# Six wide block products and one narrow one in the second MLP product, and the denominator's 1e-6 put into z

## The chip, the cores and the metric

The kernel runs on one core of a Trainium2 chip. The metric is the device time of one execution in microseconds; the time before is the median of three executions.

## The reference, cut to what matters

One transformer-like block, in float32, on 2048 tokens of 512 channels: a linear attention with 32 heads of 16 channels, and then a token-mixing MLP (2048 tokens to 1792 hidden rows and back), each behind a layer norm and with a residual.

```python
phi_q = concat([softmax(pq), softmax(-pq)])      # 32 features for each token and head
phi_k = concat([softmax(pk), softmax(-pk)])
kv  = einsum("bhsf,bhsd->bhfd", phi_k, v)
z   = einsum("bhsf->bhf", phi_k)
num = einsum("bhqf,bhfd->bhqd", phi_q, kv)
den = einsum("bhqf,bhf->bhq", phi_q, z)[..., None] + 1e-6
h   = x + merge_heads(num / den) @ wo
u   = gelu(einsum("bsd,sf->bdf", layernorm(layernorm(h)), w1) + b1)
out = h + transpose(einsum("bdf,fs->bds", u, w2) + b2)
```

The two softmaxes of a query sum to 1 each, so its 32 features sum to 2: a constant c added to each element of z adds 2c to the denominator.

## The kernel before, in words

Every matmul has float32 precision from two parts of its operands: ScalarE (ACT) rounds a tile to its high part (`hi`), VectorE (DVE) or GpSimd (POOL) subtracts to get the low part (`lo`), and the product is hi·hi + hi·lo + lo·hi, accumulated in PSUM. PSUM has eight banks of 128x512 floats.

**The attention.** Sixteen token tiles of 128 tokens go through it one after another. For each, POOL multiplies the query features by z (tile `zB`, spread over the partitions by a matmul with ones; line 503 copies it out of PSUM, line 456 multiplies), DVE reduces that per head and makes the weights `w` that normalize the features (`s_den`, lines 465 to 471: reduce, an operation that adds 1e-6 times a feature sum, multiply, reduce, reciprocal, multiply), and POOL applies them (line 474). TensorE (PE) transposes the result (line 548) and multiplies by kv and wo. Layer norm statistics and the hi and lo parts of the normalized rows (`hs`, line 62 on POOL) follow, and PE fills in with parts of the first MLP product (lines 66 to 68, output `pu`). The order on PE, DVE, ACT and POOL is written out by hand here; SP's order, which issues the loads, is left to the scheduler.

**The second MLP product** is the last stretch. Its output is made in eight stages `sp`, each for two token tiles (256 output rows). A stage sums over 1792 hidden rows in seven steps `p` of 256 rows. A step is a 2x2 block product done with seven block products in place of eight: sums of w2's blocks (`sums_of`, lines 857 to 859, DVE) and sums of u's blocks (made once) are multiplied, and sums of the seven results give the four output blocks. The table `PROD` says for each of the seven which block of w2, which block of u, which bank and which half of the bank. Two kinds exist:

- wide (`wide`, line 1106): one matmul of 512 columns, w2's high part by both parts of u, fills a whole bank, and one of 256 columns, w2's low part by u's high part, adds to its first half. The two halves have to be added when the bank is read.
- narrow (`narrow`, line 1110): three matmuls of 256 columns into one half of a bank; nothing is left to add.

Before, five products are wide and two narrow, the two narrow ones share a bank, and a stage takes six banks. The last stage uses another table, `LAST`, with seven narrow products in four banks. The banks go round: each stage takes the next ones of the eight, so that most of its banks were the previous stage's and have to be read out first. Within a stage, step 0 goes product by product in the order of the banks, the middle steps go all high parts first and then all low parts (`steps`), and the last two steps go product by product again (`products`), so that the banks finish one after another.

At the end of a stage the seven results are combined (lines 1156 to 1184): ACT copies second halves out (`e`, `low`), DVE makes the sums `e`, `u2`, `u3` and the output blocks `ot` with the bias, and POOL's queue adds `ot` and `low` to the output in memory by accumulating DMAs.

The operands of w2 come in 28 groups of two steps (`GRP`). For each group there are `sums_w2` (DVE, three additions, and the load that it may issue), `hi_w2` (ACT, line 992) and `lo_w2` (DVE, line 1002). They are called once in two steps, so at step 5 of an odd stage and at step 6 of an even one, with `lo` one group ahead of PE, `hi` two and the sums three. There are two buffers for the low parts, three for the high ones, four for the raw ones. PE, DVE and ACT run in the written order here.

Of the kernel before, what the change touches and what calls it, by code (L numbers as in the profile page):

```python
# [9 lines left out]
F32 = mybir.dt.float32  # L10
F32R = mybir.dt.float32r
AF = mybir.ActivationFunctionType
ALU = mybir.AluOpType
# [4 lines left out]
P = 128  # L18
S, D, H, DH, F = 2048, 512, 32, 16, 1792
# [10 lines left out]
Q_AT = (4, 6, 8, 9, 11, 13)  # L30
V_NOT = (0, 1, 11)
SUMS = 8
LAG = 5
WARM = 9
EPS = 1e-5
# [3 lines left out]
def block_kernel(ctx: ExitStack, tc: tile.TileContext, x, xT, wT, phic, wo, w1, b1, w2, b2,  # L39
# [9 lines left out]
    b1s = cst.tile([P, NF], F32, name="b1s")  # L49
    b2s = cst.tile([P, NT], F32, name="b2s")  # L50
    r1 = cst.tile([P, NT], F32, name="r1")
    eps2 = cst.tile([P, 1], F32, name="eps2")
    r2 = cst.tile([P, NT], F32, name="r2")
    cst.tile([P, 16], F32, name="pad")
    nc.vector.memset(ones, 1.0)
    nc.vector.memset(mhalf, -0.5)
    nc.vector.memset(eps2, EPS * EPS)

    def split(hi, lo, src, lo_engine):

# [397 lines left out]
    def s_den(t):  # L458


        tz = az.tile([P, NPR, 2, 2], F32, name="tz")
        den = az.tile([P, NPR, 2], F32, name="den")
        W[t] = az.tile([P, NPR, 2, 2], F32, name="w", bufs=3)
        other = SQ[t]
        return [lambda: nc.vector.reduce_sum(tz.rearrange("p g c h -> p (g c h)"), heads(EZ[t]), axis=AX.X),
                lambda: nc.vector.scalar_tensor_tensor(tz[:, :, 0], other[:, :, 1], 1e-6, tz[:, :, 0],
                                                       op0=ALU.mult, op1=ALU.add),
                lambda: nc.vector.tensor_mul(tz, other, tz),
                lambda: nc.vector.reduce_sum(den, tz.rearrange("p g c h -> p g h c"), axis=AX.X),
                lambda: nc.vector.reciprocal(den, den),  # L470
                lambda: nc.vector.tensor_mul(W[t], other, den.unsqueeze(2).to_broadcast([P, NPR, 2, 2]))]  # L471
# [28 lines left out]
    for g in range(2):  # L500
        pz = ps_k.tile([P, 4, P], F32, name="pk_ps")
        nc.tensor.matmul(pz, ones, zacc[:, 4 * g:4 * g + 4, :], start=True, stop=True)
        nc.scalar.activation(zB[:, 4 * g:4 * g + 4, :], pz, AF.Copy)  # L503
    q_exp(0)
    s_ez(0)
    s_ez(1)
# [92 lines left out]
    def s_moments(t):  # L599

        junk = ak.tile([P, D], F32, name="hj", bufs=1)
        if t == 0:
            ak.tile([P, 104], F32, name="end", bufs=1)
        nc.scalar.activation(VE[t][:, 1:2], VE[t][:, 2:3], AF.Copy, scale=-1.0 / D)
        nc.scalar.activation(junk, HT[t], AF.Square, bias=VE[t][:, 1:2], accum_out=VE[t][:, 3:4])
        nc.scalar.activation(VE[t][:, 0:1], VE[t][:, 3:4], AF.Identity, scale=(1.0 + EPS) / D, bias=eps2)
        if t >= NT - 2:
            nc.scalar.dma_start(out[t * P:(t + 1) * P, :], HT[t])

# [365 lines left out]
    def sums_w2():  # L975

        g = done["sums"]
        if g == NGR:
            return
        done["sums"] += 1  # L980
        if g not in RAW:
            load_w2(g)
        sums_of(RAW[g])

    def hi_w2():

        g = done["hi"]
        if g == NGR:
            return
        done["hi"] += 1  # L990
        WH[g] = keep([P, 7, GRP * P], F32R, "whi", g % 3)
        nc.scalar.activation(WH[g], RAW[g], AF.Copy)  # L992
# [92 lines left out]
    for p in range(NEAR, NP):  # L1085
# [1 line left out]
    wst.close()  # L1087
    uo = ctx.enter_context(tc.tile_pool(name="uo", bufs=2, reuse_waits="tile"))

    PROD = ((2, 1, 0, None), (5, 5, 1, None), (0, 0, 2, 0), (1, 4, 2, 1), (3, 6, 3, None), (6, 2, 4, None),  # L1090
            (4, 3, 5, None))

    def products(sp, ps, order):
        for a, b, bk, half in order:
            if half is None:
                for low in range(2):
                    for p in ps:
                        wide(sp, p, a, b, bk, low)
            else:
                for p in ps:  # L1100
                    narrow(sp, p, a, b, bk, half)
# [11 lines left out]
    def steps(sp, ps, order):  # L1113
        for p in ps:
            for a, b, bk, half in order:
                if half is None:
                    wide(sp, p, a, b, bk, 0)
        for p in ps:
            for a, b, bk, half in order:
                if half is None:  # L1120
                    wide(sp, p, a, b, bk, 1)
            for a, b, bk, half in order:
                if half is not None:
                    narrow(sp, p, a, b, bk, half)
# [6 lines left out]
    for n, (sp, p) in enumerate(STEPS):  # L1131
        t = 2 * sp
        last = t + 2 == NT
        if n % GRP == 0 and p < NP - 1:
            lo_w2()
            hi_w2()
            sums_w2()
        if p == 0:
            bank = []
            for _ in range(6):  # L1140
                pool = (ps_f, ps_q, ps_b, ps_b)[n_bank % 8 // 2]
                bank.append(pool.tile([P, 2, HD], F32, name="py", tag="pu"))
                n_bank += 1
        order = LAST if last else PROD
        run_on = 3 if last else 2
        if p == 0:
            products(sp, [p], order)
            continue
        if p < NP - run_on:
            if n % GRP == 0 or p == 1:  # L1150
                steps(sp, range(p, min(p + GRP - n % GRP, NP - run_on)), order)
            continue
        if p < NP - 1:
            continue
        products(sp, range(NP - run_on, NP), order)
        e = uo.tile([P, 2, HD], F32, name="e")
        u2 = uo.tile([P, HD], F32, name="u2", bufs=1)
        u3 = uo.tile([P, HD], F32, name="u3")
        if not last:
            ot = uo.tile([P, 2, 2, HD], F32, name="ot", bufs=1)  # L1160
            low = uo.tile([P, 3, HD], F32, name="low")
            nc.scalar.activation(e[:, 1], bank[0][:, 0], AF.Copy)
            for i in range(3):
                nc.scalar.activation(low[:, i], bank[3 + i][:, 1], AF.Copy)
            nc.vector.tensor_add(e[:, 1], bank[0][:, 1], e[:, 1])
            nc.vector.tensor_sub(u2, bank[1][:, 0], e[:, 1])
            nc.vector.tensor_add(u2, bank[1][:, 1], u2)
            nc.vector.tensor_sub(u3, u2, bank[2][:, 0])
            nc.vector.scalar_tensor_tensor(e[:, 0], bank[2][:, 1], -1.0, u2, op0=ALU.mult, op1=ALU.subtract)

            def out_block(i, h, o, add):
                nc.vector.scalar_tensor_tensor(ot[:, i, h], o, b2s[:, t + i:t + i + 1], add, op0=ALU.add, op1=ALU.add)  # L1172

            out_block(0, 0, bank[2][:, 1], u3)
            out_block(0, 1, bank[3][:, 0], u3)
            nc.gpsimd.dma_start(out[t * P:(t + 1) * P, :], flat(ot[:, 0]), accum_op=ALU.add)  # L1176
            if n % GRP == 0:
                lo_w2()
                hi_w2()
            out_block(1, 0, bank[4][:, 0], e[:, 0])  # L1180
            out_block(1, 1, bank[5][:, 0], e[:, 1])
            nc.gpsimd.dma_start(out[(t + 1) * P:(t + 2) * P, :], flat(ot[:, 1]), accum_op=ALU.add)
            nc.gpsimd.dma_start(out[t * P:(t + 1) * P, HD:D], low[:, 0], accum_op=ALU.add)
            nc.gpsimd.dma_start(out[(t + 1) * P:(t + 2) * P, :], flat(low[:, 1:3]), accum_op=ALU.add)
            if n % GRP == 0:
                sums_w2()
            continue

        hb = [uo.tile([P, 2, HD], F32, name=f"hb{i}", bufs=1) for i in range(2)]
        for i in range(2):  # L1190
            nc.sync.dma_start(flat(hb[i]), out[(t + i) * P:(t + i + 1) * P, :])
            nc.vector.tensor_scalar(hb[i], hb[i], b2s[:, t + i:t + i + 1], None, op0=ALU.add)
        nc.scalar.activation(e[:, 1], bank[0][:, 0], AF.Copy)
        nc.vector.tensor_add(hb[1][:, 1], bank[0][:, 0], hb[1][:, 1])
        nc.vector.tensor_sub(u2, bank[0][:, 1], e[:, 1])
        nc.vector.tensor_sub(hb[1][:, 0], hb[1][:, 0], u2)
        nc.vector.tensor_sub(u3, u2, bank[1][:, 0])
        nc.vector.tensor_add(hb[0], hb[0], u3.unsqueeze(1).to_broadcast([P, 2, HD]))
        nc.vector.tensor_add(hb[0][:, 0], bank[1][:, 1], hb[0][:, 0])
        nc.vector.tensor_sub(hb[1][:, 0], hb[1][:, 0], bank[1][:, 1])  # L1200
        nc.vector.tensor_add(hb[0][:, 1], bank[2][:, 0], hb[0][:, 1])
        nc.sync.dma_start(out[t * P:(t + 1) * P, :], flat(hb[0]))
        for k, o, q in ((0, bank[2][:, 1], nc.scalar), (1, bank[3][:, 0], nc.sync)):
            nc.vector.tensor_add(hb[1][:, k], o, hb[1][:, k])
            q.dma_start(out[(t + 1) * P:NT * P, k * HD:(k + 1) * HD], hb[1][:, k])
# [49 lines left out]
```

## Time and profile before

| what | value |
|---|---|
| median of 3 executions | 518.52 us (518.47 to 518.72) |
| the profiled execution | 518.56 us; span of its instructions 516.8 us |
| PE matmuls | 510.9 us busy, 99% of the span, 3595 matmuls |
| PE weight loads | 442.9 us, 86% |
| DVE | 445.5 us, 86% |
| ACT | 296.8 us, 57% |
| POOL | 245.0 us, 47% |
| granted PE clock | 1.0 throughout |

The span runs from the first to the last instruction of the program; the rest of the execution, 518.56 - 516.8 = 1.76 us, lies around it. An engine's busy time in the table is a mean over stages with different limits. A matmul's recorded duration is longer than the distance to the next matmul, since matmuls overlap: what a matmul costs is read from the distance of starts, not from its duration.

### The profile page before, as it was taken

What the parts mean: (1) busy time and instruction counts of PE and PEld (TensorE: products, weight loads), DVE (VectorE), ACT (ScalarE), POOL (GpSimd) and SP (SyncE); (2) the same over time, 40 slices, a digit from 0 to 9 for tenths busy, and PEclk for the clock granted to TensorE, in tenths of its full rate; (3) what the DMA queues carried; (4) which work ended last, traced back from release to release, by engine and by line L of the source; (5) the groups of instructions that cost most, each with busy time, mean ns of one, the idle gap of its engine ahead of it and who ended that gap; (6) DMA issues with size and microseconds to landing.
All of it is one profiled execution on the core that took longest, in us unless ns stands there. A gap on an engine that the chain in (4) does not pass through costs nothing.

```text
span 516.8 us, 9476 instructions
## 1 busy us (share of the span) xinstructions
PE 510.9 (99%) x3595; PEld 442.9 (86%) x3595; DVE 445.5 (86%) x789; ACT 296.8 (57%) x494; POOL 245.0 (47%) x188
## 2 busy tenths in 40 slices
PE   9999999999999999999999999999999999999997
PEld 8888888887877778777788899998889999899997
DVE  6893999986799998777796998989989898988985
ACT  6998944434255876668976643457653434434430
POOL 2479799975999999985343200000002212212220
PEclk9999999999999999999999999999999999999999
DMA  8744310000041324334322233374135787677843
GB/s 313 270 127 122 81 53 29 1 1 3 12 154 41 103 84 140 124 124 122 115 89 83 82 105 104 99 245 141 43 123 117 162 192 171 119 162 159 191 50 77
DMA packets 36300, 58.56 MB, mean 113 GB/s; under 512 B 3744, under 2 KB 19360, under 8 KB 36256
## 3 DMA queue, kind: packets, MB, share of 16 engines
q1 hardware_dynamic: 31648, 50.85, 31.3%
q0 software_dynamic: 4032, 6.42, 9.9%
q8 instruction: 28, 0.46, 0.4%
q10 hardware_dynamic: 576, 0.69, 0.4%
q14 instruction: 16, 0.13, 0.1%
HBM read 46.81 MB, written 11.14 MB: 112 GB/s over the span
## 4 chain that ended last, share of the span: by engine, by line
PE 89%; POOL 7%; DVE 2%; ACT 1%; issue 1%; POOLq 0%
PE py L1106 17%; PE pu L936 12%; PE py L1110 10%; PE pu L66 7%; PE pu L67 7%; PE pu L68 7%; PE pv L67 3%; PE pv L68 3%; PE pv L66 3%; PE pk_ps L66 2%; PE pk_ps L68 2%; PE pk_ps L67 2%; POOL ez L456 2%; POOL eq L474 2%; PE po L68 2%; PE tn L548 2%
## 5 line engine op out<-in xcount | busy, mean ns | idle before, releaser
L1176 POOL DMA_DIRECT2D out<-ot x7 | 6.2, 884 | 142.1 <-DVE ot L1172 142.1
L992 ACT ACTIVATE whi<-wraw 128x1792 fp32r<-128x1792 f32 x28 | 47.6, 1701 | 44.1 <-DVE wraw L859 20.3
L1002 DVE TENSOR_TENSOR wlo<-wraw,whi 128x1792 fp32r<-128x1792 f32 x28 | 56.6, 2021 | 8.4 <-PE py L1110 6.9
L67 PE MATMUL pu<-hs,whi 128*128 128x512 f32 x128 | 50.3, 393 | 1.2 <-POOL hs L62 1.2
L66 PE MATMUL pu<-hs,whi 128*128 128x512 f32 x128 | 50.1, 399 | 0.0
L1106 PE MATMUL py<-uf,whi 128*128 128x512 f32 x175 | 48.4, 393 | 0.0
L68 PE MATMUL pu<-hs,wlo 128*128 128x512 f32 x128 | 48.0, 390 | 0.0
L897 ACT ACTIVATE whi<-wraw 128x896 fp32r<-128x896 f32 x24 | 22.9, 954 | 31.2 <-PE pu L936 26.4
L456 POOL TENSOR_TENSOR ez<-eq,zB 128x1024 f32<-128x1024 f32 x16 | 38.3, 2399 | 4.4 <-ACT zB L503 4.4
L1110 PE MATMUL py<-uf,whi 128*128 128x256 f32 x210 | 39.0, 283 | 0.0
L936 PE MATMUL pu<-ht,whi 128*128 128x256 f32 x192 | 35.6, 283 | 0.0
L208 POOL TENSOR_TENSOR pk<-pk,sk 128x1024 f32<-128x1024 f32 x16 | 30.9, 1938 | 7.3 <-DVE sk L207 7.2
L62 POOL TENSOR_TENSOR hs<-hb,hs 128x512 fp32r<-128x512 f32 x16 | 22.4, 1400 | 23.9 <-ACT hs L61 23.8
L550 ACT ACTIVATE pht<-tn 128x512 f32<-128x512 f32 x32 | 17.4, 595 | 28.4 <-PE tn L548 28.3
L474 POOL TENSOR_TENSOR eq<-eq,w 128x1024 f32<-128x1024 f32 x16 | 32.4, 2028 | 1.3 <-DVE w L471 1.2
L1110 PEld LDWEIGHTS py<-uf,whi 128*128 128x128 f32 x210 | 32.7, 192 | 0.0
L1106 PEld LDWEIGHTS py<-uf,whi 128*128 128x128 f32 x175 | 29.8, 189 | 3.5
L212 POOL TENSOR_TENSOR zacc<-zacc,pk 128x1024 f32<-128x1024 f32 x13 | 31.2, 2399 | 0.5
L1106 PEld LDWEIGHTS py<-uf,wlo 128*128 128x128 f32 x175 | 27.9, 190 | 4.0
L66 PEld LDWEIGHTS pu<-hs,whi 128*128 128x128 f32 x128 | 24.1, 188 | 7.2 <-issue 2.5
L936 PEld LDWEIGHTS pu<-ht,whi 128*128 128x128 f32 x192 | 30.0, 192 | 0.0
L1110 PE MATMUL py<-uf,wlo 128*128 128x256 f32 x105 | 29.7, 283 | 0.0
(207 smaller groups left out, 1625.0 us busy)
## 6 DMA issues: line engine op xcount, KB each, us to landing
wraw<-in_w SPq DMA_DIRECT2D x28, 512.0 KB, 4.5
wraw<-in_w SPq DMA_DIRECT2D x48, 256.0 KB, 2.8
xraw<-in_xT SPq DMA_DIRECT2D x16, 256.0 KB, 3.1
xh<-in_x SPq DMA_DIRECT2D x16, 256.0 KB, 2.7
h<-in_x SPq DMA_DIRECT2D x16, 256.0 KB, 2.7
out<-h SPq DMA_DIRECT2D x14, 256.0 KB, 2.7
out<-ot POOLq DMA_DIRECT2D x14, 256.0 KB, 4.8
wraw<-in_wT SPq DMA_DIRECT2D x12, 256.0 KB, 4.6
```

The source lines that it names most:

```text
L66: nc.tensor.matmul(o, ah, bh, start=first, stop=False)
L67: nc.tensor.matmul(o, ah, bl, start=False, stop=False)
L68: nc.tensor.matmul(o, al, bh, start=False, stop=last)
L208: nc.gpsimd.tensor_mul(heads(PK[t]), heads(PK[t]), sk.unsqueeze(2).to_broadcast([P, 2 * H, DH]))
L212: nc.gpsimd.tensor_add(zacc, zacc, PK[t])
L456: nc.gpsimd.tensor_mul(EZ[t], EQ[t], zB)
L474: nc.gpsimd.tensor_mul(heads(EQ[t]), heads(EQ[t]), W[t].rearrange("p g c h -> p (g c h)").unsqueeze(2).to_broadcast([P, 2 * H, DH]))
L936: nc.tensor.matmul(ACC[p][bk][:, half], WS[p, i][x][:, a], hb[b][y], start=i == 0 and half == 0 and k == 0, stop=i == NT // 2 - 1 and k == ...
L992: nc.scalar.activation(WH[g], RAW[g], AF.Copy)
L1002: nc.vector.tensor_sub(wl_, RAW[g], WH[g])
L1106: nc.tensor.matmul(o, w, u, start=p == 0 and not low, stop=p == NP - 1, skip_group_check=True)
L1110: nc.tensor.matmul(bank[bk][:, half], AW[sp, p][x][:, a], UB[p, b][:, y], start=p == 0 and half == 0 and i == 0, stop=p == NP - 1 and i == ...
```

## The change

Product 0 becomes wide and gets a bank of its own: six wide products, one narrow, seven banks for a stage in place of six. One more DVE operation in a stage (line 1174 after) subtracts the second half of its bank; the copies and output blocks read banks with other numbers. In the first stage the last product of step 0 moves behind step 1, because its bank still holds a result of the first MLP product. The sums of w2 that were called at step 5 of an odd stage move behind the stage's output blocks, and at the end of an even stage `lo` and `hi` move from between the two pairs of output blocks to behind them, except in the stage before the last.

In the attention the operation that adds 1e-6 (line 466) goes, and the copy of z out of PSUM becomes one that adds 0.5e-6 to each element, with the constant from a second column of the tile `eps2`.

```diff
@@ constants
-    eps2 = cst.tile([P, 1], F32, name="eps2")
+    eps2 = cst.tile([P, 2], F32, name="eps2")
...
-    nc.vector.memset(eps2, EPS * EPS)
+    nc.vector.memset(eps2[:, :1], EPS * EPS)
+    nc.vector.memset(eps2[:, 1:], DEN_EPS / 2)
@@ s_den
         return [lambda: nc.vector.reduce_sum(tz.rearrange("p g c h -> p (g c h)"), heads(EZ[t]), axis=AX.X),
-                lambda: nc.vector.scalar_tensor_tensor(tz[:, :, 0], other[:, :, 1], 1e-6, tz[:, :, 0],
-                                                       op0=ALU.mult, op1=ALU.add),
                 lambda: nc.vector.tensor_mul(tz, other, tz),
@@ zB
-        nc.scalar.activation(zB[:, 4 * g:4 * g + 4, :], pz, AF.Copy)
+        nc.scalar.activation(zB[:, 4 * g:4 * g + 4, :], pz, AF.Identity, bias=eps2[:, 1:])
@@ second MLP product
-    PROD = ((2, 1, 0, None), (5, 5, 1, None), (0, 0, 2, 0), (1, 4, 2, 1), (3, 6, 3, None), (6, 2, 4, None),
-            (4, 3, 5, None))
+    PROD = ((2, 1, 0, None), (5, 5, 1, None), (0, 0, 2, None), (1, 4, 3, 0), (3, 6, 4, None), (6, 2, 5, None),
+            (4, 3, 6, None))
...
         if n % GRP == 0 and p < NP - 1:
             lo_w2()
             hi_w2()
-            sums_w2()
+            if p < NP - 2 or last:
+                sums_w2()
...
-            for _ in range(6):
+            for _ in range(4 if last else 7):
...
-            products(sp, [p], order)
+            products(sp, [p], order[:-1] if n == 0 else order)
+            continue
+        if n == 1:
+            steps(sp, [p], order[:-1])
+            products(sp, [0, p], order[-1:])
             continue
...
             for i in range(3):
-                nc.scalar.activation(low[:, i], bank[3 + i][:, 1], AF.Copy)
+                nc.scalar.activation(low[:, i], bank[4 + i][:, 1], AF.Copy)
...
             nc.vector.tensor_sub(u3, u2, bank[2][:, 0])
-            nc.vector.scalar_tensor_tensor(e[:, 0], bank[2][:, 1], -1.0, u2, op0=ALU.mult, op1=ALU.subtract)
+            nc.vector.tensor_sub(u3, u3, bank[2][:, 1])
+            nc.vector.scalar_tensor_tensor(e[:, 0], bank[3][:, 0], -1.0, u2, op0=ALU.mult, op1=ALU.subtract)
...
-            out_block(0, 0, bank[2][:, 1], u3)
-            out_block(0, 1, bank[3][:, 0], u3)
+            out_block(0, 0, bank[3][:, 0], u3)
+            out_block(0, 1, bank[4][:, 0], u3)
...
-            if n % GRP == 0:
+            ahead = t + 4 == NT
+            if ahead:
                 lo_w2()
                 hi_w2()
-            out_block(1, 0, bank[4][:, 0], e[:, 0])
-            out_block(1, 1, bank[5][:, 0], e[:, 1])
+            out_block(1, 0, bank[5][:, 0], e[:, 0])
+            out_block(1, 1, bank[6][:, 0], e[:, 1])
+            if n % GRP == 0 and not ahead:
+                lo_w2()
+                hi_w2()
...
-            if n % GRP == 0:
-                sums_w2()
+            sums_w2()
```

The order of the instructions shows the move at two places. On DVE, at the end of the second stage (names: `wraw` the raw blocks of a group and their sums, `wlo` their low part, `e`, `u`, `ot` as above), before:

```order
L1002 TENSOR_TENSOR wlo_4756<-wraw,whi 128x1792
L857 TENSOR_TENSOR wraw<-wraw 128x512
L858 TENSOR_TENSOR wraw<-wraw 128x256
L859 TENSOR_TENSOR wraw<-wraw 128x256
L1165 TENSOR_TENSOR e<-py,e 128x256
L1166 TENSOR_TENSOR u_4798<-py,e 128x256
L1167 TENSOR_TENSOR u_4798<-py,u_4798 128x256
L1168 TENSOR_TENSOR u_4799<-u_4798,py 128x256
L1169 SCALAR_TENSOR_TENSOR e<-py,u_4798 128x256
L1172 SCALAR_TENSOR_TENSOR ot<-py,b2s,u_4799 128x256 x2
L1172 SCALAR_TENSOR_TENSOR ot<-py,b2s,e 128x256 x2
```

The same place on DVE after:

```order
L1002 TENSOR_TENSOR wlo_4732<-wraw,whi 128x1792
L1170 TENSOR_TENSOR e<-py,e 128x256
L1171 TENSOR_TENSOR u_4767<-py,e 128x256
L1172 TENSOR_TENSOR u_4767<-py,u_4767 128x256
L1173 TENSOR_TENSOR u_4768<-u_4767,py 128x256
L1174 TENSOR_TENSOR u_4768<-u_4768,py 128x256
L1175 SCALAR_TENSOR_TENSOR e<-py,u_4767 128x256
L1178 SCALAR_TENSOR_TENSOR ot<-py,b2s,u_4768 128x256 x2
L1178 SCALAR_TENSOR_TENSOR ot<-py,b2s,e 128x256 x2
L857 TENSOR_TENSOR wraw<-wraw 128x512
L858 TENSOR_TENSOR wraw<-wraw 128x256
L859 TENSOR_TENSOR wraw<-wraw 128x256
```

The three sums moved from ahead of the output blocks to behind them, and one subtraction came in between.

On PE, step 0 of the second stage (`py` the banks, `un` the parts of u for steps 0 and 1), its third and fourth product before, both in bank `py_4654`:

```order
L1106 MATMUL py_4653<-un0_3275,whi_4526 128x512
L1106 MATMUL py_4653<-un0_3275,wlo1_4564 128x256
L1110 MATMUL py_4654<-un0_3275,whi_4526 128x256 x2
L1110 MATMUL py_4654<-un0_3275,wlo1_4564 128x256
L1110 MATMUL py_4654<-un0_3275,whi_4526 128x256 x2
L1110 MATMUL py_4654<-un0_3275,wlo1_4564 128x256
L1106 MATMUL py_4655<-un0_3275,whi_4526 128x512
```

The same place on PE after:

```order
L1106 MATMUL py_4633<-un0_3260,whi_4510 128x512
L1106 MATMUL py_4633<-un0_3260,wlo1_4546 128x256
L1106 MATMUL py_4634<-un0_3260,whi_4510 128x512
L1106 MATMUL py_4634<-un0_3260,wlo1_4546 128x256
L1110 MATMUL py_4635<-un0_3260,whi_4510 128x256 x2
L1110 MATMUL py_4635<-un0_3260,wlo1_4546 128x256
L1106 MATMUL py_4636<-un0_3260,whi_4510 128x512
```

Three matmuls of 256 columns became one of 512 and one of 256, in a bank of their own.

More of the change, by code (lines that the diff above doesn't have):

```diff
@@ L32 @@
 SUMS = 8
+DEN_EPS = 1e-6
 LAG = 5
@@ L605, in s_moments @@
         nc.scalar.activation(junk, HT[t], AF.Square, bias=VE[t][:, 1:2], accum_out=VE[t][:, 3:4])
-        nc.scalar.activation(VE[t][:, 0:1], VE[t][:, 3:4], AF.Identity, scale=(1.0 + EPS) / D, bias=eps2)
+        nc.scalar.activation(VE[t][:, 0:1], VE[t][:, 3:4], AF.Identity, scale=(1.0 + EPS) / D, bias=eps2[:, :1])
         if t >= NT - 2:
```

## The prediction

> **What bounds the kernel now.** I read the page's header and its chain of waits first, then TensorE's (PE) own rows in the second MLP product, then the engines that release its banks there, and last the few places in the attention where PE waits.
>
> ```profile
> span 516.8 us, 9476 instructions
> ...
> PE 89%; POOL 7%; DVE 2%; ACT 1%; issue 1%; POOLq 0%
> ```
>
> The chain that ends last runs through PE for 89% of the span, through GpSimd (POOL) for 7% and VectorE (DVE) for 2%. The profiled execution took 518.56 us, 1.76 us more than its span and 0.04 us more than the median of 518.52; the sum below is made against 518.56. What a measurement of this kernel can tell from no change is 0.2%, or 1.04 us.
>
> Two windows are an odd stage of the second MLP product and the even stage behind it. Columns: the window, its length, busy time and number of instructions of PE, weight loads, DVE, ScalarE (ACT) and POOL, granted clock, DMA share, GB/s.
>
> ```profile
> 395.20:412.40 17.20, 17.20 (x113) 15.74 (x112) 15.42 (x25) 8.12 (x8) 3.34 (x4) 1.00 0.74 170
> 412.40:429.60 17.20, 17.20 (x113) 15.68 (x113) 15.59 (x23) 6.54 (x7) 3.59 (x5) 1.00 0.77 156
> ```
>
> PE is busy through both, at full clock. DVE has 1.6 to 1.8 us of a stage left: it is the engine that an added operation can push over the edge. So a stage gets shorter by fewer or cheaper matmuls, and longer if DVE gives a bank back late.
>
> **A narrow and a wide product.** PE's rows at the end of that odd stage, by start, duration and line:
>
> ```profile
> 405.99 0.40 PE L1110 MATMUL py<-uf,whi 128*128 128x256 f32 x2
> ...
> 407.43 0.63 PE L1106 MATMUL py<-uf,whi 128*128 128x512 f32 x2
> ...
> 409.52 0.40 PE L1106 MATMUL py<-un,whi 128*128 128x512 f32 x1
> ```
>
> Durations overlap, so I take distances of starts. From 405.99 to 407.43 PE does four narrow products (two products in each of the last two steps): 1.44 / 4 = 0.360 us each, 0.120 for each of three matmuls of 256 columns. From 407.43 to 409.52 it does six wide ones (three products, two steps): 2.09 / 6 = 0.348 us each. Both pass 768 columns; the wide one has one matmul and one weight load fewer. The change makes one narrow product in a step wide, in seven steps of seven stages (the last stage keeps its table): 49 x 0.012 = 0.59 us, I take **-0.6**. All of it is on the path, since PE is without a gap there. Bounds: nothing, if the wide form gains only where it stands among other wide ones, and 0.6.
>
> A rule of the Trainium skill speaks against this gain: "TensorE: Matmul & The Clock Gate", section "Back-to-back issue gap", gives an isolated matmul's spacing at full clock as its columns over 2.4, in ns, plus about 2.5 ns. By that formula 327.5 ns stand against 325.0, and the estimate from it is 49 x 2.5 ns = 0.12 us, a sum of 518.4; the trace disagrees with its fixed part, since 0.360 and 0.348 us are the measured distances.
>
> **Does DVE give the banks back in time?** DVE's rows at the same place; `wlo` is the low part of w2, lines 857 to 859 the sums, the rest the combination of the seven results:
>
> ```profile
> 404.87 2.03 DVE L1002 TENSOR_TENSOR wlo<-wraw,whi 128x1792 fp32r<-128x1792 f32 x1 [1.26 <-PE py L1110]
> 406.81 0.68 DVE L857 TENSOR_TENSOR wraw<-wraw 128x512 f32<-128x512 f32 x1
> ...
> 408.33 0.42 DVE L1165 TENSOR_TENSOR e<-py,e 128x256 f32<-128x256 f32 x1
> 408.86 0.42 DVE L1166 TENSOR_TENSOR u<-py,e 128x256 f32<-128x256 f32 x1
> 409.31 0.42 DVE L1167 TENSOR_TENSOR u<-py,u 128x256 f32<-128x256 f32 x1
> 409.84 0.42 DVE L1168 TENSOR_TENSOR u<-u,py 128x256 f32<-128x256 f32 x1
> 410.18 0.42 DVE L1169 SCALAR_TENSOR_TENSOR e<-py,u 128x256 f32<-128x256 f32 x1
> 410.52 0.87 DVE L1172 SCALAR_TENSOR_TENSOR ot<-py,b2s,u 128x256 f32<-128x256 f32 x2
> 411.30 0.87 DVE L1172 SCALAR_TENSOR_TENSOR ot<-py,b2s,e 128x256 f32<-128x256 f32 x2
> ```
>
> With seven banks of eight, bank k of the next stage is bank k-1 of this one, for k from 1 to 6; its bank 0 is the eighth. The next stage's first matmul starts at 409.52, and a wide product takes 0.348 us, so the six old banks are wanted at 409.87, 410.21, 410.56, 410.92, 411.27 and 411.62.
>
> The change takes the sums (406.81 to 408.33, 1.52 us) out of the way, so the combination starts when `wlo` is done, at 406.81; ACT's copy that it needs is done by then (next fence). With the distances of these rows (0.53, 0.45, 0.53, then 0.34 or 0.39) and 0.45 for the added subtraction (nearest row: line 1168, 0.42 long), its ten operations start at 406.81, 407.34, 407.79, 408.32, 408.77, 409.11, 409.45, 409.84, 410.23 and 410.62. The last reader of each bank is then done at about 407.2, 408.2, 409.2, 409.9, 410.3 and 410.7: ahead of the want by 2.7, 2.0, 1.4, 1.0, 1.0 and 0.9 us. **Cost of the added operation: nothing**, hidden by DVE's idle time; the removed 1.52 us is the cover. Without it the last bank would come 1.52 - 0.9 = 0.6 us late, once for each of the three odd stages.
>
> ACT's copies are paced by PE and stay where they are:
>
> ```profile
> 406.34 0.36 ACT L1162 ACTIVATE e<-py 128x256 f32<-128x256 f32 x1
> ...
> 409.72 0.38 ACT L1164 ACTIVATE low<-py 128x256 f32<-128x256 f32 x1 [0.31 <-PE py L1106]
> ```
>
> The last ends at 410.10, ahead of 410.62. The moved sums go behind the outputs, 411.0 to 412.5, with the next `wlo` behind them: a delay of 0.4 us against 412.08 before, from the added operation alone. In an even stage the change puts `wlo` behind the last pair of outputs:
>
> ```profile
> 426.87 2.03 DVE L1002 TENSOR_TENSOR wlo<-wraw,whi 128x1792 fp32r<-128x1792 f32 x1 [0.38 <-PE py L1106]
> 428.81 0.87 DVE L1172 SCALAR_TENSOR_TENSOR ot<-py,b2s,e 128x256 f32<-128x256 f32 x2
> ```
>
> The next stage starts at 426.78 there, so the two banks that these outputs read, freed at 429.2 and 429.6, would be wanted at about 428.5 and 428.9 and come late; put first, the outputs end near 427.8. `wlo` then starts 0.95 us later and ends near 429.8; PE wants it after the first two steps (a group), 2 x (5 x 0.348 + 2 x 0.360) = 4.9 us into the stage, at 431.7. The accumulating DMAs that leave with the outputs on POOL's queue move with them, with nothing but other stores behind them; the loads that `sums` issues on SP's queue go three groups ahead, 3 x 4.9 = 15 us, so a few us are nothing. Cost: nothing, with 1.9 us of cover.
>
> In the first stage one product waits for a bank that ACT's gelu reads last:
>
> ```profile
> 377.26 1.37 ACT L800 ACTIVATE u<-pu,b1s 128x512 f32<-128x512 f32 x2 [4.72 <-PE pu L68]
> 377.74 1.07 PE L1106 MATMUL py<-un,whi 128*128 128x512 f32 x4
> ```
>
> The gelus end at 378.63; with the product moved behind the next step PE has over 1.5 us of other matmuls from 377.74 (one step is 2.46). Nothing, again.
>
> **The attention.** The groups of the removed operation (line 466), of a copy without and with a bias on ACT (lines 604 and 606), and of POOL's line 62; busy time, then the mean in ns:
>
> ```profile
> L62 POOL TENSOR_TENSOR hs<-hb,hs 128x512 fp32r<-128x512 f32 x16 | 22.4, 1400 | 23.9 <-ACT hs L61 23.8
> ...
> L606 ACT ACTIVATE ve<-ve,eps 128x1 f32<-128x1 f32 x16 | 4.7, 295 | 0.5
> ...
> L604 ACT ACTIVATE ve<-ve 128x1 f32<-128x1 f32 x16 | 3.0, 188 | 0.0
> L466 DVE SCALAR_TENSOR_TENSOR tz<-smq,tz 128x32 f32<-128x32 f32 x16 | 3.0, 187 | 0.3
> ```
>
> POOL's waits there, what it does before PE's one gap, and the gap, from the rows by time:
>
> ```profile
> 152.77 1.94 POOL L474 TENSOR_TENSOR eq<-eq,w 128x1024 f32<-128x1024 f32 x1 [0.47 <-DVE w L471]
> ...
> 164.70 0.55 POOL L611 TENSOR_TENSOR r<-ve,mhalf 128x1 f32<-128x1 f32 x1 [0.67 <-ACT ve L606]
> ...
> 186.44 1.74 POOL L62 TENSOR_TENSOR hs<-hb,hs 128x512 fp32r<-128x512 f32 x1
> ...
> 188.23 0.50 PE L67 MATMUL pu<-hs,whi 128*128 128x512 f32 x1 [1.17 <-POOL hs L62]
> ```
>
> The removal takes 16 x 0.187 = 3.0 us from DVE, nearly all off the path: POOL waits for the weights `w` once, 0.47 us at 152.77. Part of that goes, but at 164.70 POOL waits again, 0.67 us, for ACT's statistics, which PE paces; that sets POOL's time anew. The only gap in PE's rows there, 1.17 us at 188.23, hangs on POOL's chain from then on. I take **0**; bounds -1.17 (gap closed) and +0.4 (POOL's rows lie otherwise to DVE's: `L62` took 1.74 here, 1.40 in the mean, 0.34 more). The copy with a bias is bounded by line 606 against 604, 0.107 us for each of two copies, between 0 and +0.2.
>
> Sum: 518.56 - 0.6 + 0 = 517.96; 0.04 off for the median, **517.9 us**. The forecast's own bounds are 517.9 - 0.1 and 517.9 + 0.6 (0.4 and 0.2).
>
> **The rivals.**
>
> - *POOL's chain moves up and the gap at 188 closes.* For it: DVE loses an operation in each tile, and the last of POOL's operations before the gap took 1.74 us where their mean is 1.40, so 0.34 of the 1.17 could go with another neighbour on DVE. Against: the wait for ACT at 164.70 lies between. Time: 517.9 - 1.17 = 516.7; a gap that half closes gives 517.3.
> - *The wide product saves nothing,* because the distance is set by the columns (768 in both) and the 0.012 us belong to neighbours of the same kind. Against: four narrow ones in a row hold 0.360 and six wide ones 0.348 at the same clock. Time: 518.5, to 518.7 with the bias. The formula of "TensorE: Matmul & The Clock Gate" in the Trainium skill would come out close to this.
> - *Slower: a bank comes back late at the stage boundaries.* Place: line 1106 or 1110 of a stage's first step, waiting for DVE line 1172. Seven banks of eight leave one bank of lead where six left two, and DVE's work grows by 0.42 to about 16.0 of 17.1 us. It decides once DVE's combination runs more than 0.9 us behind the schedule above: the start of `wlo` at 404.87 waits for PE (1.26 us), and every shift there passes on to the whole chain. Price: 0.6 us at three boundaries gives 517.9 + 1.8 = 519.7; at all six 521.5; 1 us at all six 523.9. Against: every margin worked out is 0.9 us or more. The Trainium skill, "Perfetto Trace Analysis", section "Optimization Strategy", says that a gap repeating on an engine that should be full can mean too few buffers in PSUM for the next tile; no such gap is in the rows before.
>
> **How the numbers follow.** Forecast 0.50, no saving 0.07, gap closed 0.25 (0.05 of it beyond 516.7, with other waits of PE or POOL going too), a late bank 0.18. Faster by over 0.2% means under 517.48: the gap closed, 0.25. Slower means over 519.56: the late bank, 0.18. Within: 0.57. The range takes in the forecast, no saving and the gap closed from 516.7 on; that leaves out 0.05 + 0.18, over 0.2, so it reaches to the cheapest late bank, 519.7.
>
> **What would show it.** Right: stages 0.08 us shorter (7 x 0.012), line 1106 up by 49 twice and line 1110 down by 147, no wait on PE at a stage's first step, DVE's first combining operation directly behind `wlo` in odd stages, the gap near 188 still there. Wrong: a wait of PE for line 1172 or 1164, a stage as long as before, or a gap near 188 that is gone or much larger.

## The result and the profile after

The changed kernel takes 517.53 us (median of 11 runs, 517.09 to 518.14) against 518.47 (11 runs, 518.03 to 519.19) for the kernel before on the same chip: ratio 0.9984, 95% interval 0.9976 to 0.9991. That is 0.83 us less (0.47 to 1.24). The forecast was 517.9, with -0.6 for the wide products and 0 for the attention; the sign, the place and the mechanism hold, the size came out a little larger. By the forecast's own measure of 0.2% (1.04 us) it is still the outcome "within", to which it gave 0.57; the interval nevertheless lies clear of 1.

The first matmuls of the second, third and fourth stage after, from PE's rows by time:

```profile
391.86 0.40 PE L1106 MATMUL py<-un,whi 128*128 128x512 f32 x1
...
409.01 0.40 PE L1106 MATMUL py<-un,whi 128*128 128x512 f32 x1
...
426.15 0.40 PE L1106 MATMUL py<-un,whi 128*128 128x512 f32 x1
```

A stage takes 17.15 or 17.14 us where it took 17.24 or 17.26. PE is without a gap in those two stages, and DVE has more to do (16.0 us in the mean of the two, 15.5 before), with the same columns as in the windows before:

```profile
394.70:411.85 17.15, 17.15 (x106) 15.37 (x106) 15.53 (x26) 6.54 (x7) 3.45 (x4) 1.00 0.77 174
411.85:429.00 17.15, 17.15 (x106) 15.35 (x106) 16.44 (x24) 8.24 (x8) 3.45 (x5) 1.00 0.67 148
```

DVE at the end of the same odd stage, line numbers of the kernel after (1174 is the added subtraction, 1178 the output blocks):

```profile
404.39 2.03 DVE L1002 TENSOR_TENSOR wlo<-wraw,whi 128x1792 fp32r<-128x1792 f32 x1 [1.06 <-PE py L1110]
406.33 0.42 DVE L1170 TENSOR_TENSOR e<-py,e 128x256 f32<-128x256 f32 x1
...
408.30 0.42 DVE L1174 TENSOR_TENSOR u<-u,py 128x256 f32<-128x256 f32 x1
408.63 0.42 DVE L1175 SCALAR_TENSOR_TENSOR e<-py,u 128x256 f32<-128x256 f32 x1
408.97 0.87 DVE L1178 SCALAR_TENSOR_TENSOR ot<-py,b2s,u 128x256 f32<-128x256 f32 x2
409.75 0.87 DVE L1178 SCALAR_TENSOR_TENSOR ot<-py,b2s,e 128x256 f32<-128x256 f32 x2
410.54 0.68 DVE L857 TENSOR_TENSOR wraw<-wraw 128x512 f32<-128x512 f32 x1
```

This is the written schedule, shifted by 0.5 us with the stage: 406.81 became 406.33, 408.77 became 408.30, 410.23 became 409.75, and the sums follow.

In the attention POOL's two waits and PE's one gap stand where they stood:

```profile
152.29 1.94 POOL L474 TENSOR_TENSOR eq<-eq,w 128x1024 f32<-128x1024 f32 x1 [0.41 <-DVE w L471]
...
164.49 0.55 POOL L611 TENSOR_TENSOR r<-ve,mhalf 128x1 f32<-128x1 f32 x1 [0.95 <-ACT ve L606]
...
188.02 0.50 PE L69 MATMUL pu<-hs,whi 128*128 128x512 f32 x1 [1.17 <-POOL hs L64]
```

POOL came to its operation near 152 earlier by 0.48 us, 0.28 more than the 0.20 us by which this whole run is ahead (see below), and lost the 0.28 at 164 in a wait for ACT that is longer by as much (0.95 against 0.67). PE's gap is still 1.17 us.

**Where the profiled difference went.** 518.56 against 517.50 us, 1.06 less. PE's hundredth matmul (counted from 0) starts at 17.85 before and 17.66 after: 0.20 us of the difference lie ahead of it, in the start of the run, which differs from run to run (last section). From there to the first matmul of the second MLP product, 336.2 us, the two differ by 0.02. The first stage is 0.20 shorter (38.04 against 38.24) and the six after it together 0.64; the last stage and what follows it are the same.

### The profile page after: what moved, and what is told of

Read it like the earlier page. It is cut to its first block, busy times and chain, and to the rows that moved or that the text cites. A ratio compares the mean times of both kernels' runs of the same rounds, so it can differ in the third digit from the quotient of the medians.

```text
span 515.7 us, 9378 instructions
## 1 busy us (share of the span) xinstructions
PE 509.7 (99%) x3546; PEld 439.6 (85%) x3546; DVE 447.0 (87%) x781; ACT 297.3 (58%) x494; POOL 244.7 (47%) x188
## 4 chain that ended last, share of the span: by engine, by line
PE 91%; POOL 3%; DVE 2%; ACT 2%; DMA 1%; issue 0%; SPq 0%; POOLq 0%; ACTq 0%
PE py L1106 20%; PE pu L936 12%; PE pu L68 8%; PE pu L69 8%; PE pu L70 8%; PE py L1110 7%; PE pv L69 3%; PE pv L70 3%; PE pv L68 3%; PE pk_ps L68 3%; PE pk_ps L69 2%; PE pk_ps L70 2%; PE tn L548 2%; PE po L70 2%; PE po L69 2%; PE po L68 2%
## 5 line engine op out<-in xcount | busy, mean ns | idle before, releaser
L1106 PE MATMUL py<-uf,whi 128*128 128x512 f32 x210 | 57.6, 394 | 0.0
L1106 PEld LDWEIGHTS py<-uf,whi 128*128 128x128 f32 x210 | 35.8, 189 | 4.3
L1106 PEld LDWEIGHTS py<-uf,wlo 128*128 128x128 f32 x210 | 33.1, 190 | 4.6
L1106 PE MATMUL py<-uf,wlo 128*128 128x256 f32 x210 | 35.0, 281 | 0.0
L68 PEld LDWEIGHTS pu<-hs,whi 128*128 128x128 f32 x128 | 24.1, 188 | 7.1 <-issue 2.5
L69 PEld LDWEIGHTS pu<-hs,whi 128*128 128x128 f32 x128 | 24.1, 188 | 6.6 <-POOL hs L64 2.1
L70 PEld LDWEIGHTS pu<-hs,wlo 128*128 128x128 f32 x128 | 23.9, 188 | 4.8
```

The source lines that it names most:

```text
L68: nc.tensor.matmul(o, ah, bh, start=first, stop=False)
L69: nc.tensor.matmul(o, ah, bl, start=False, stop=False)
L70: nc.tensor.matmul(o, al, bh, start=False, stop=last)
L1106: nc.tensor.matmul(o, w, u, start=p == 0 and not low, stop=p == NP - 1, skip_group_check=True)
```

## The experiments

Stage lengths are distances between the first matmuls of stages, in the profiled run; stages count from 0, and those after stage 2 repeat stages 1 and 2 in turn. Medians are over 5 to 11 runs; the kernel before ran beside them with medians of 518.47 (changed), 518.33 (the next four), 518.18 (the four after) and 518.11 (the last two). "To 100" is the start of PE's hundredth matmul, counted from 0.

| kernel | us | ratio to before, 95% interval | to 100 | stage 0 | stage 1 | stage 2 | last |
|---|---|---|---|---|---|---|---|
| before | 518.47 | | 17.85 | 38.24 | 17.24 | 17.26 | 17.51 |
| changed | 517.53 | 0.9984 (0.9976 to 0.9991) | 17.66 | 38.04 | 17.15 | 17.14 | 17.51 |
| attention only | 518.55 | 1.0002 (0.9993 to 1.0011) | 17.87 | 38.24 | 17.24 | 17.26 | 17.51 |
| products only | 517.74 | 0.9992 (0.9984 to 1.0001) | 17.43 | 38.04 | 17.15 | 17.14 | 17.51 |
| seven banks, narrow | 518.41 | 0.9999 (0.9990 to 1.0008) | 17.23 | 38.21 | 17.24 | 17.26 | 17.51 |
| seven wide | 516.94 | 0.9973 (0.9963 to 0.9984) | 17.68 | 37.99 | 17.05 | 17.07 | 17.63 |
| sums kept | 520.05 | 1.0035 (1.0023 to 1.0048) | 17.93 | 38.04 | 17.15 | 17.96 | 17.51 |
| low part between | 518.93 | 1.0017 (1.0008 to 1.0025) | 18.15 | 38.04 | 17.70 | 17.14 | 17.51 |
| two more on DVE | 517.74 | 0.9993 (0.9984 to 1.0002) | 17.44 | 38.04 | 17.15 | 17.26 | 17.51 |
| four more on DVE | 520.48 | 1.0045 (1.0033 to 1.0058) | 17.42 | 38.04 | 17.15 | 18.19 | 17.51 |
| changed, again | 517.41 | 0.9985 (0.9976 to 0.9994) | 17.32 | 38.04 | 17.15 | 17.14 | 17.51 |
| seven wide, low part earlier | 517.07 | 0.9978 (0.9969 to 0.9987) | 17.28 | 37.99 | 17.05 | 17.07 | 17.51 |

**The two parts, each alone.** The attention part on the kernel before:

```diff
-                lambda: nc.vector.scalar_tensor_tensor(tz[:, :, 0], other[:, :, 1], 1e-6, ...
-        nc.scalar.activation(zB[...], pz, AF.Copy)
+        nc.scalar.activation(zB[...], pz, AF.Identity, bias=eps2[:, 1:])
```

> The kernel before with the attention part alone (1e-6 in z, no operation per token tile). Theory A, the gain is the wide product's: no change, 518.5 us within 0.3, stages of 17.25 us, POOL still re-timed by ACT's statistics near 164.5 and the gap of PE near 188 still 1.17 us. Theory B, the attention part gives its share: 0.3 to 0.5 us less, with the gap near 188 shorter.

And the changed kernel with these lines turned back:

> The changed kernel with the attention as before (the operation of 1e-6 back, the copy of z without a bias). Theory A: the whole gain is there, 517.6 us, stages of 17.14 us. Theory B: 518.0, the rest missing.

The first is the kernel before in time and in every stage. Its profile has POOL's two waits as in the changed kernel (0.40 us at 152.49, 0.95 us for ACT at 164.69) and PE's gap of 1.16 us at 188.24: the attention part alone ends in the wait for ACT. The second has every stage of the changed kernel. Its time alone would not decide (the interval touches 1), but its stages do: the gain is all in the second MLP product.

**Banks and places without the wide product.**

```diff
-    PROD = (..., (0, 0, 2, None), (1, 4, 3, 0), ...
+    PROD = (..., (0, 0, 2, 0), (1, 4, 3, 0), ...
-            nc.vector.tensor_sub(u3, u3, bank[2][:, 1])
```

> The changed kernel with its seven banks, its new places for sums and low parts, but product 0 narrow in its own bank, and without the added subtraction. Theory A, fewer matmuls make the gain: stages are 17.25 us again and the time is 518.4. Theory C, the longer turn of the banks or the moved DVE work makes it: stages of 17.14 us, 517.6.

Stages of 17.24 and 17.26 us: the longer turn of the banks and the moved DVE work bring nothing in a full stage; with the product moved behind step 1 they bring 0.03 of the first stage's 0.20. So the form of product 0, one matmul and one weight load fewer in each step, makes the gain; which of the two counts was not separated.

**What the moves are for.** The sums back ahead of the combination:

```diff
-            if p < NP - 2 or last:
-                sums_w2()
+            sums_w2()
...
-            sums_w2()
+            if n % GRP == 0:
+                sums_w2()
```

> The changed kernel with the sums of w2 back at step 5 of the odd stages, ahead of the combination. Theory A, the moved sums are the cover of the added operation: the last bank comes 0.6 us late at three boundaries, the odd stages' successors take 17.75 us in place of 17.14, 517.5 + 1.8 = 519.3, and PE waits for line 1178. Rival, the cover isn't needed: 517.5.

The stages behind odd ones take 17.96 us, 0.82 longer, at three boundaries: 2.4 us, and the median is 2.5 above the changed kernel's. DVE's chain and PE at such a boundary (here 1173 is the added subtraction):

```profile
410.11 0.42 DVE L1173 TENSOR_TENSOR u<-u,py 128x256 f32<-128x256 f32 x1
...
410.78 0.87 DVE L1177 SCALAR_TENSOR_TENSOR ot<-py,b2s,u 128x256 f32<-128x256 f32 x2
411.56 0.87 DVE L1177 SCALAR_TENSOR_TENSOR ot<-py,b2s,e 128x256 f32<-128x256 f32 x2
```

```profile
410.22 0.28 PE L1106 MATMUL py<-un,wlo 128*128 128x256 f32 x1
410.67 0.48 PE L1110 MATMUL py<-un,whi 128*128 128x256 f32 x2 [0.17 <-DVE u L1173]
...
411.31 0.50 PE L1106 MATMUL py<-un,whi 128*128 128x512 f32 x1
411.64 0.28 PE L1106 MATMUL py<-un,wlo 128*128 128x256 f32 x1
411.76 0.44 PE L1106 MATMUL py<-un,whi 128*128 128x512 f32 x1
```

The added subtraction starts at 410.11 and ends at 410.53; PE goes on at 410.67, 0.56 us after its start. Behind it the products start 0.64 and 0.45 us apart where 0.35 or 0.36 is PE's own pace. So the slower rival exists where the forecast put it; the first bank to be late is the one that the added subtraction frees, not the last.

The weight loads (PEld) show the wait more closely than the matmuls. Here are the loads for the fifth and the seventh product of this step:

```profile
411.31 0.19 PEld L1106 LDWEIGHTS py<-un,whi 128*128 128x128 f32 x1 [0.25 <-DVE ot L1177]
...
412.09 0.19 PEld L1106 LDWEIGHTS py<-un,whi 128*128 128x128 f32 x1
```

And here is the load for the seventh product in the changed kernel, where nothing waits:

```profile
410.99 0.19 PEld L1106 LDWEIGHTS py<-un,whi 128*128 128x128 f32 x1
```

Each of the two late loads starts 0.53 us after the start of the output block that frees its bank (410.78 and 411.56). In the changed kernel the load for the seventh product starts 0.12 us ahead of its matmul (411.11) and 1.98 us into the stage; here it starts 412.09 - 409.29 = 2.80 us into it. That is 0.82 us later, as much as the stage is longer. So the bank has to be free in time for the weight load, and the load comes before the matmul.

The low part back between the output blocks:

```diff
-            ahead = t + 4 == NT
+            ahead = n % GRP == 0
```

> The changed kernel with the low part of w2 back between the two pairs of output blocks in the even stages. Theory A: two banks wanted 1.7 and 2.1 us into the next stage come free 2.4 and 2.8 us into it, 0.7 us late at three boundaries: 517.5 + 2.1 = 519.6. Rival, PE wants them later than worked out: 517.5.

The stages behind even ones are longer by 0.55 us (17.70 against 17.15), not by 0.7. DVE and PE at the first such boundary; the stage starts at 392.37:

```profile
392.46 2.03 DVE L1002 TENSOR_TENSOR wlo<-wraw,whi 128x1792 fp32r<-128x1792 f32 x1
394.40 0.87 DVE L1178 SCALAR_TENSOR_TENSOR ot<-py,b2s,e 128x256 f32<-128x256 f32 x2
```

```profile
394.12 0.39 PE L1106 MATMUL py<-un,whi 128*128 128x512 f32 x1
394.35 0.28 PE L1106 MATMUL py<-un,wlo 128*128 128x256 f32 x1
394.93 0.50 PE L1106 MATMUL py<-un,whi 128*128 128x512 f32 x1 [0.30 <-DVE ot L1178]
```

One bank is late, the seventh product's: it starts at 394.93, 0.53 us after the start of the output block that frees it, and 0.81 us after the sixth product in place of 0.35. Its weight load also starts at 394.93, 2.56 us into the stage where the changed kernel has 1.98.

**How much room DVE has.** Scratch operations at the head of the combination in odd stages, two and four:

```diff
+            for _ in range(2 * (sp % 2)):
+                nc.vector.tensor_add(x, x, x)
             nc.vector.tensor_add(e[:, 1], bank[0][:, 1], e[:, 1])
```

The kernel with four has 4 in place of the 2. In these two kernels, and in those with seven wide products, the tile `u3` has one buffer in place of two.

> The changed kernel with two further DVE operations of 0.42 us (a scratch tile added to itself) at the head of the combination in the three odd stages. The chain moves by 0.9 us, the margin worked out: theory A, no or hardly any wait of PE, 517.5 to 517.8. Rival, the true margin is much smaller or DVE as a whole is full: 0.4 us or more at each of the three boundaries, 518.7 or more.

> The same with four further operations: the chain moves by 1.8 us, 0.9 more than the margin. Theory A: PE waits 0.9 us at each of three boundaries, 517.5 + 2.7 = 520.2. Rival, a larger margin: 517.5 to 518.5.

With two, stages behind odd ones are 0.12 us longer; with four, 1.05. The scratch operations push the chain back by 0.80 us (406.17 to 406.97) and by 1.71 us (406.17 to 407.88), a little less than the 0.9 and 1.8 expected. From two to four the chain moves by 0.91 us and the stage by 0.93: one for one, and back from there the room is 0.66 to 0.68 us (1.71 - 1.05 and 0.80 - 0.12), not 0.9. PE's row where it first waits, with four (1178 is the added subtraction, which ends at 409.85 + 0.42 = 410.27):

```profile
409.85 0.42 DVE L1178 TENSOR_TENSOR u<-u,py 128x256 f32<-128x256 f32 x1
```

```profile
410.41 0.47 PE L1110 MATMUL py<-un,whi 128*128 128x256 f32 x2 [0.36 <-DVE u L1178]
```

Again there are 0.56 us from DVE's start to PE's matmul, and 0.53 us to the load of its weights (410.38). The forecast counted 0.42, the operation's own time, and held it against the start of the matmul. With 0.53 us up to the load, the last bank's room in the changed kernel is 410.99 - (409.75 + 0.53) = 0.71 us, close to the 0.66 to 0.68 that the scratch operations show.

**A step further: seven wide products.** Product 1 has a bank to itself already:

```diff
-    PROD = (..., (1, 4, 3, 0), ...
+    PROD = (..., (1, 4, 3, None), ...
+            nc.scalar.activation(x, bank[3][:, 1], AF.Copy)
...
+            nc.vector.tensor_add(x, bank[3][:, 0], x)
-            nc.vector.scalar_tensor_tensor(e[:, 0], bank[3][:, 0], -1.0, u2, ...
+            nc.vector.scalar_tensor_tensor(e[:, 0], x, -1.0, u2, ...
-            out_block(0, 0, bank[3][:, 0], u3)
+            out_block(0, 0, x, u3)
```

> The changed kernel with product 1 wide too, so seven wide ones in the same seven banks; ACT copies the second half of its bank (0.38 us) and DVE adds the first half to it (0.42 us, one more operation in the chain). Theory A: 49 more matmuls gone, stages of 17.03 us, 0.75 us less than the changed kernel, 516.8; the bank margins fall from 0.9 to about 0.5 us and still hold. Rival, DVE is now too late (16.4 of 17.0 us busy): PE waits for the output blocks at the start of a stage, 0.2 us or more at up to six boundaries, 517.6 or more.

Stages of 17.05 and 17.07 us, no wait for a bank: 0.08 less a stage in the mean, not 0.11, and the last stage is 0.12 longer. There PE reaches the low part before DVE has made it (494.92 + 2.02 = 496.94):

```profile
494.92 2.02 DVE L1002 TENSOR_TENSOR wlo<-wraw,whi 128x1792 fp32r<-128x1792 f32 x1
```

```profile
496.72 0.40 PE L1110 MATMUL py<-un,whi 128*128 128x256 f32 x2
496.99 0.39 PE L1110 MATMUL py<-un,wlo 128*128 128x256 f32 x1
497.21 0.28 PE L1110 MATMUL py<-un,whi 128*128 128x256 f32 x1
```

So the low part was put one output block earlier there:

```diff
+            if ahead:
+                lo_w2()
+                hi_w2()
             out_block(0, 1, bank[4][:, 0], u3)
...
-            if ahead:
-                lo_w2()
-                hi_w2()
```

> Seven wide products as before, and in the stage before the last the low part of w2 (and ACT's high part) one output block earlier, since the last stage was 0.12 us longer with seven wide ones, where PE waited for that low part in its second step. Theory A: the last stage is back at 17.51 us, the others stay at 17.06, 0.5 to 0.6 us less than the changed kernel. Rival: the last stage's 0.12 us have another cause and stay.

> The changed kernel once more, to stand beside the next one on the same chip: 517.5 us, stages of 17.14 us.

The last stage is back at 17.51. From the first to the last matmul of the second MLP product the three kernels take 158.41 (changed, both times), 158.00 and 157.88 us. By the medians side by side seven wide products with the earlier low part take 0.34 us less than the changed kernel, 517.07 against 517.41; those intervals overlap, and PE's rows, 0.53 us apart, are the better witness.

## Why the prediction was right

- *Wide against narrow.* The mechanism is shown by the kernel with seven banks and a narrow product. The term was mis-sized: 0.012 us a product was read at the end of a stage, where PE's rows after still give the same (0.348 for the wide ones); over a whole stage (17.25 - 17.143) / 7 = 0.015. The second conversion, to seven wide, gives (17.143 - 17.063) / 7 = 0.011. The distances of starts of all matmuls in stages 1 and 2 take the 0.015 apart: a narrow product takes 359 ns and a wide one 349 in the mean before, 357 and 349 after. The converted product itself so gives 7 x 10.5 ns = 0.07 of the 0.11 us a stage. The other 0.03 lie in the six that kept their form and got a little shorter, the narrow one by 2 ns and each wide one by half a ns; the forecast left them as they were, and why they are closer stays open. The rival "saves nothing" fell. The Trainium skill gives in "TensorE: Matmul & The Clock Gate", section "Back-to-back issue gap", a spacing for an isolated matmul whose fixed part is 2.5 ns; the estimate from it was 0.12 us. The second product's rows give 0.84, so the measurement decides against using that spacing here.
- *The first stage.* Forecast like the others; it gave 0.20 in place of 0.08. The moved product, the banks and the moved DVE work together account for 0.03 (38.24 to 38.21 with a narrow product), the wide one for 0.17. By the distances of starts 0.11 of the 0.20 lie in the second product's own matmuls, as in the other stages, and 0.09 in the 92 matmuls of the first MLP product that are mixed in: they follow each other at 227.5 ns in the mean where it was 228.4. Why these are closer stays open.
- *The cover.* The working of the ten operations held to 0.05 us, and "0.6 us late at three boundaries" without the moved sums was measured as 0.82. The step at fault took the bank as free 0.42 us after its last reader's start and as wanted at the matmul's start; 0.53 us pass before the weight load, which has its place 0.12 us ahead of the matmul. That is 0.53 + 0.12 - 0.42 = 0.23 us less room, and 0.6 + 0.23 = 0.83. The Trainium skill says in "Perfetto Trace Analysis", section "Optimization Strategy", that a gap repeating on an engine that should be full can mean too little room in PSUM for the next tile. The gap does repeat, at all three boundaries; but it goes with the same seven of eight banks, once DVE frees them earlier.
- *The low part.* The forecast had two banks late by 0.7 us. It mislaid one bank: by its own rule the bank of the last output block isn't wanted in the next stage at all, and the one before it is wanted at 428.88 and freed at 429.23, 0.35 late, 0.58 with the 0.23 from above. Measured: 0.58 at that product's weight load (2.56 - 1.98) and 0.55 in the stage.
- *The attention.* Nothing, as forecast, and by the wait named: what DVE gave POOL went at 164 into the wait for ACT. The rival with 0.25, that the gap near 188 closes, fell; each of the two copies with the bias took 687 ns in place of 598 and POOL waited 4.5 us for them in place of 4.4, but the stretch up to the second MLP product is not longer for it.

The time moved by 0.94 us between the two medians (0.83 by the ratio), 0.3 more than forecast: 0.24 of it by the terms above, the rest within what the start of a run changes.

## What to carry to other kernels

Where PE was full, a matmul and its weight load fewer for the same columns were worth 11 to 15 ns each. The gain was kept only because the engine that frees the PSUM banks got the room first: the moved sums and low part are worth 2.4 and 1.7 us, more than the gain that they protect. Work out such a cover bank by bank, the last reader's start plus 0.53 us (measured here for 256 columns on DVE) against the start of the next writer's weight load, and then test it by putting scratch work on that engine until PE waits. An operation taken off an engine that another one re-timed later moved nothing here.

## What the runs showed that was not expected

PE's hundredth matmul starts anywhere from 17.23 to 18.15 us in kernels that are the same up to there but for a constant. The stretch from there to the second MLP product repeats to 0.09 us, and equal stages to 0.02. In the first 18 us DVE waits 4.0 us for two loads in the run with the latest start, 3.0 in the kernel before and 2.8 in the run with the earliest, so loads have a part in it. So 0.9 us of scatter between runs lies in the first 17 us, and a change of half a microsecond is read more safely from distances in the trace than from a few whole times.
